# Attention and two feed-forward nets on one core: warm-up products on halves of TensorE's array

## The chip, the core and the metric

The kernel runs on one core of one Trainium2 chip. The metric is the device time of one execution in microseconds. Before the change it is 760.52 us, the median of three runs (759.41 to 760.74). Everything below is read from one further execution that was taken with the hardware profiler.

## What is computed

Three steps follow one another on 1152 tokens (2 x 576) of width 512. First, attention with 8 heads of 64 columns and a rotary embedding of q and k:

```python
def rotate(x):
    x1, x2 = (x[..., :half], x[..., half:])
    return np.concatenate([x1 * cos - x2 * sin, x1 * sin + x2 * cos], axis=-1)
q_rot, k_rot = (rotate(q), rotate(k))
scores = scale * np.matmul(q_rot, k_rot.transpose(0, 1, 3, 2))
...
attn = np.exp(scores)
attn = attn / (np.sum(attn, axis=-1, keepdims=True) + 1e-09)
return np.matmul(attn, v).astype(np.float32)
```

Then a mixture of 4 experts (512 to 1024, relu, back to 512), weighted by `domain_probs`, and last a net of 512 to 2048 to 512 with a leaky relu of slope 0.01.

## The kernel before

Attention goes over 8 pairs of heads. For each pair, the transposed q and k are loaded (L219), multiplied by the two tables `tab` (L229, two products), summed (L232), split into a rounded part (L268 on ACT, L270 on POOL) and a rest (L253, L255), and put together into `stk`. A score tile (L312) is a group of products into PSUM; DVE takes its negative maximum (L329), ACT the exponential (L339), TensorE turns it (L395, L401, L402), ACT and DVE split it (L420, L424), and it is multiplied with v (L472). Each multiplied operand is a sum of two float32r parts.

For the first pair the loads are cut in pieces so that work starts early: k in two halves of 288 columns, q in 192 and 384 columns. POOL and DVE share the rotary products and sums of these pieces.

Two small operands matter below. `VZ` holds, for two pairs in turn, the 64 left-over rows of v for both heads; it must be zero outside its blocks, so both are zeroed once (task `vz_zero`, L671, POOL), and the blocks are filled later (L284, L285). `stk` of the first pair needs zeros too (L316 on POOL, L317 on DVE). `ident` is the identity that turns tiles; POOL makes it first.

Nearly all instructions stand in tasks of a planner (`Plan`): each task names its engines, its cost and what it follows, and the planner writes down one order for each engine, which the engines then follow strictly. Waits between engines are put in from the tiles that instructions read and write: a write to a tile waits for all its earlier readers on other engines. What stands ahead of the planner in the code (`ident` and the warm-up products of TensorE, L629 to L631) stands ahead of its tasks in each engine's order too. The warm-up is `WARM` = 22 float32 products of `ident` with itself, into one PSUM tile that is not read:

```python
t = ps_a.tile([P, P], F32, tag="t", name="warm")
for _ in range(WARM):
    pe.matmul(t, lhsT=ident, rhs=ident, start=True, stop=True)
...
vz_zero = task("zero", 0, lambda e: [pool.memset(f32(z), 0.0) for z in VZ], [("POOL", 0.8)], ())
```

Of the kernel before, what the change touches and what calls it, by code (L numbers as in the profile page):

```python
# [11 lines left out]
F32 = mybir.dt.float32  # L12
# [8 lines left out]
P = 128  # L21
# [10 lines left out]
EARLY = 3  # L32
ON_DVE = (0, 1, 2, 3, 8, 9)
FH = FU // 2
WARM = 22


RANK = {"tab_q": [2043.63, 1989.1, 2043.63], "zero": [1293.68, 1391.39, 1354.79], "load_x1": [1391.71, 1675.91, 1893.96], "load_x0": [1434.91,
# [118 lines left out]
def f32(ap):  # L157
    return ap.bitcast(F32)
# [3 lines left out]
def attention_then_two_ffns(ctx, tc, xqk, vp, rope, dprob, w1, w2, w_in, w_out, out):  # L162
# [4 lines left out]
    pe, dve, act, pool, sp = nc.tensor, nc.vector, nc.scalar, nc.gpsimd, nc.sync  # L167
# [5 lines left out]
    ident = const.tile([P, P], F32, name="ident")  # L173
# [22 lines left out]
    def opened(name, bufs, **kw):  # L196
        return att.enter_context(tc.tile_pool(name=name, bufs=bufs, **kw))
# [5 lines left out]
    ps_s, ps_a, ps_b = (opened(n, 2, space=PSUM) for n in ("ps_s", "ps_a", "ps_b"))  # L203
# [5 lines left out]
    VZ = [tab_p.tile([P, 2, 2, D], F32R, name=f"vz{i}") for i in range(2)]  # L209
# [47 lines left out]
    def stack(p, w, h, part):  # L257

        stk, hl = stk_of(p), HL[p]
        src, dst = slice(64 * h, 64 * h + 64), slice(64 * part, 64 * part + 64)  # L260
        if w == 0:
            sp.dma_start(f32(stk[dst, h, 0]), f32(hl[src, part, 0]))
        else:
            sp.dma_start(f32(stk[dst, h, 1:3]), f32(hl[src, :, 1]))
# [30 lines left out]
    def chunk(i):  # L295
        return (0, i * P) if i < 2 else (0, 2 * P) if i == KT else (1, (i - 2) * P)
# [291 lines left out]
    def half_1(v, f, c):  # L588
        if (v, f) not in HP:
            HP[v, f] = ps_b.tile([P, 512], F32, tag="t", name=f"hp{v}_{f}")  # L590
        w, x = HW[v, 0], xT[0]
        for k, (l, r) in enumerate(((0, 1), (0, 0), (1, 0))):
            pe.matmul(HP[v, f], lhsT=w[:, c, l, f * P:(f + 1) * P], rhs=x[:, r, c], start=(c, k) == (0, 0), stop=(c, k) == (NC - 1, 2))  # L593
# [10 lines left out]
    def half_2(v, i):  # L604
        ps = HY[v, i] = ps_b.tile([P, DM], F32, tag="t", name=f"hy{v}_{i}")
        h, w, ts_ = HX[v], HW[v, 1], slice(i * P, (i + 1) * P)
        ops = []
        for f in range(FH // P):
            ops += [(h[:, 0, f, ts_], w[:, f, 1]), (h[:, 0, f, ts_], w[:, f, 0]), (h[:, 1, f, ts_], w[:, f, 0])]
        products(ps, ops)  # L610
# [15 lines left out]

    with tc.manual_schedule():

        t = ps_a.tile([P, P], F32, tag="t", name="warm")  # L629
        for _ in range(WARM):  # L630
            pe.matmul(t, lhsT=ident, rhs=ident, start=True, stop=True)  # L631
        plan = Plan()
        add = plan.add
        rings = {k: Ring(v) for k, v in {"x": 3, "hl": 1, "stk": 2, "v": 1, "vs": 2, "p": 2, "pl": 1, "s": 2, "ta": 2, "tb": 2, "pt0": 1, "pt1": 1,
# [17 lines left out]
        def task(kind, n, fn, choices, after):  # L652

            return add(fn, [(e, us, MORE[kind] if j else 0) for j, (e, us) in enumerate(choices)], after, rank_of(kind, n))
# [6 lines left out]
        def transfer(kind, n, fn, kb, after):  # L661
            return dma(fn, kb, after, rank_of(kind, n), 0.48 if "load" in kind else 0.65, MORE[kind] if kind in ("load_x0", "load_x1", "load_tab") and n < 1 else None)
# [20 lines left out]
        for p in range(NP_ALL):  # L683
# [4 lines left out]
            for w, nm in ((1, "xk"), (0, "xq")):  # L688
# [20 lines left out]
                for h in range(2 if p else 0):  # L709
                    for part in range(2):  # L710
                        t = transfer(f"stack{w}", n0 + .1 * h, lambda p=p, w=w, h=h, part=part: stack(p, w, h, part), 148 * (1 + w), lo_of[-1] + stk_w)
# [25 lines left out]
            for n in range(n0, n0 + PER):  # L737
                _, i, h = ORDER[n]
                big = i < KT
                c, _ = chunk(i)  # L740
# [75 lines left out]
        for v in range(2 * AHEAD):  # L816
# [13 lines left out]
            for f in range(FH // P):  # L830
                b_t, b_w = fresh("tb")
                t = None
                for c in range(NC):
                    need = [t] if c else parts[0][1] + x_done + b_w
                    t = task("half_1", 4 * v + f, lambda e, v=v, f=f, c=c: half_1(v, f, c), [("PE", 0.69)], need)
# [5 lines left out]
            for i in range(BLOCKS[0][1] // P):  # L841
                b_t, b_w = fresh("tb")
                t = task("half_2", 4 * v + 2, lambda e, v=v, i=i: half_2(v, i), [("PE", 1.37)], h_done + parts[1][1] + b_w)
# [311 lines left out]
        for c in (B11, T3, B21, B22):  # L1155
            d = plan.add(lambda e: None, [("X", 0.0 if c in (B11, T3) else 8.5, 0)], [], -99)
# [80 lines left out]
```

## Time and profile before

| | us |
|---|---|
| median of the runs | 760.52 |
| profiled execution | 759.67 |
| its span, first to last instruction | 757.7 |
| PE (TensorE products) busy | 728.2 (96%) |
| DVE busy | 527.0 (70%) |
| ACT busy | 422.0 (56%) |
| POOL busy | 385.9 (51%) |
| span granted at full TensorE clock, mean | 0.998 |

The busy shares are means over the whole span. Attention takes about its first 235 us, the two nets the rest. The engines' names: PE is TensorE, PEld its weight load, DVE VectorE, ACT ScalarE, POOL GpSimd, SP the engine that issues most transfers.

### The profile page before, as it was taken

The page shows a single profiled execution, that of the slowest core. Times are in us where ns is not written, and L with a number is a line of the kernel's source. Part 1 is how long each engine was busy: PE and PEld are TensorE (multiplying, and loading weights), DVE is VectorE, ACT ScalarE, POOL GpSimd, SP SyncE. Part 2 cuts the span into 40 slices and gives each one's busy share as a digit, 9 for nine tenths or more (in the row PEclk, how much of TensorE's full clock was granted, in tenths as well). Part 3 has the DMA queues.
Part 4 walks back from the last instruction along what each step waited for, and adds up shares of the span by engine and source line. Part 5 has one row for each costly group of instructions (what it writes and reads, how often), then busy time and mean ns, then how long its engine had stood idle before and what let it go on. Part 6 is the DMA issues. An engine that isn't in the chain of part 4 may idle for free.

```text
span 757.7 us, 12165 instructions
## 1 busy us (share of the span) xinstructions
PE 728.2 (96%) x4396; PEld 654.1 (86%) x4396; DVE 527.0 (70%) x927; ACT 422.0 (56%) x1017; POOL 385.9 (51%) x386
## 2 busy tenths in 40 slices
PE   6789899999999999999999999998999999999998
PEld 6678788888888988898998989888889899898997
DVE  7899988677776888986666666867769844243342
ACT  5688885666553464574472744735448447082540
POOL 7887876656267000246574763935004628475440
PEclk9999999999999999999999999999999999999999
DMA  8665646355042133454544533646101120000002
GB/s 261 166 189 168 158 106 173 114 140 122 29 167 93 47 112 97 138 172 138 158 144 146 190 128 91 202 153 220 58 1 57 33 80 29 28 29 1 1 29 97
DMA packets 40811, 84.55 MB, mean 112 GB/s; under 512 B 4656, under 2 KB 9520, under 8 KB 40752
## 3 DMA queue, kind: packets, MB, share of 16 engines
q1 hardware_dynamic: 39936, 83.00, 36.0%
q10 hardware_dynamic: 816, 0.79, 0.3%
q8 instruction: 34, 0.56, 0.3%
q14 instruction: 25, 0.20, 0.1%
HBM read 60.64 MB, written 10.75 MB: 94 GB/s over the span
## 4 chain that ended last, share of the span: by engine, by line
PE 85%; DVE 6%; POOL 3%; ACT 2%; DMA 2%; issue 1%; SPq 1%; ACTq 0%; POOLq 0%; DVEq 0%
PE start L472 35%; PE seeded L520 17%; PE start L520 12%; PE hp L593 4%; PE hy L472 4%; PE s L312 4%; PE o L472 3%; PE t L395 3%; PE seeded L527 1%; DVE pt L424 1%; DVE nm L329 1%; DMA x<-in_xqk_dram 1%; DMA tab<-in_rope_dram 1%; POOL x L232 1%; POOL hw L586 1%
## 5 line engine op out<-in xcount | busy, mean ns | idle before, releaser
L472 PE MATMUL start<-w,h 128*128 128x512 f32 (+1 forms) x1164 | 268.6, 388 | 0.0
L472 PEld LDWEIGHTS start<-w,h 128*128 128x128 f32 x1164 | 215.2, 188 | 42.9 <-DVE g L1024 0.2
L990 POOL TENSOR_TENSOR rest<-raw,rest 128x512 int32<-128x512 int32 x32 | 42.8, 1336 | 124.8 <-PE start L472 54.2
L914 POOL TENSOR_TENSOR h<-g,h 128x256 fp32r<-128x256 f32 (+1 forms) x64 | 53.9, 859 | 85.4 <-ACT h L1025 79.7
L268 ACT ACTIVATE w<-raw 128x512 fp32r<-128x512 f32 x81 | 50.3, 628 | 74.1 <-PE start L472 66.4
L914 POOL TENSOR_TENSOR w<-raw,w 128x512 fp32r<-128x512 f32 x46 | 64.0, 1401 | 41.0 <-ACT w L268 24.3
L520 PE MATMUL seeded<-xt,w 128*128 128x256 f32 (+1 forms) x480 | 74.3, 298 | 2.9 <-ACT seeded L1062 2.9
L520 PE MATMUL start<-xT,w 128*128 128x320 f32 (+1 forms) x480 | 74.7, 298 | 1.5 <-POOL w L914 0.9
L550 DVE SCALAR_TENSOR_TENSOR acc<-start,prob,acc 128x512 f32<-128x512 f32 x55 | 41.1, 749 | 48.0 <-PE start L472 47.9
L520 PEld LDWEIGHTS seeded<-xt,w 128*128 128x128 f32 x480 | 68.2, 189 | 4.4 <-ACT seeded L1062 3.7
L520 PE MATMUL seeded<-xT,w 128*128 128x320 f32 (+1 forms) x480 | 71.4, 298 | 0.5 <-ACT seeded L1062 0.5
L520 PEld LDWEIGHTS start<-xT,w 128*128 128x128 f32 x480 | 67.9, 190 | 2.6 <-POOL w L914 1.1
L520 PEld LDWEIGHTS seeded<-xT,w 128*128 128x128 f32 x480 | 67.2, 189 | 1.8 <-ACT seeded L1062 1.0
L420 ACT ACTIVATE pt<-t 128x384 fp32r<-128x384 f32 (+2 forms) x128 | 53.3, 440 | 25.6 <-PE t L395 22.4
L424 DVE TENSOR_TENSOR pt<-t,pt 128x384 fp32r<-128x384 f32 (+2 forms) x128 | 60.1, 492 | 8.7 <-ACT pt L420 7.2
L312 PE MATMUL s<-stk 128*128 128x288 f32 x288 | 53.3, 315 | 7.9 <-ACT p L339 5.4
L339 ACT ACTIVATE p<-s,nm 128x576 f32<-128x576 f32 x72 | 53.3, 740 | 13.0 <-DVE nm L329 12.4
L554 DVE TENSOR_TENSOR acc<-start,acc 128x512 f32<-128x512 f32 (+1 forms) x28 | 18.8, 673 | 54.5 <-PE start L472 54.5
L329 DVE TENSOR_REDUCE nm<-s 128x1 f32<-128x576 f32 x72 | 53.6, 749 | 4.0 <-PE s L312 3.3
L395 PE MATMUL t<-ident,p 128*128 128x128 f32 x288 | 45.4, 275 | 8.9 <-ACT p L339 3.4
L312 PEld LDWEIGHTS s<-stk 128*128 128x128 f32 x288 | 41.6, 192 | 12.1 <-ACT p L339 7.9
L1062 ACT ACTIVATE seeded<-seeded 128x320 f32<-128x320 f32 (+1 forms) x80 | 32.0, 400 | 33.0 <-PE seeded L520 32.1
(134 smaller groups left out, 1355.8 us busy)
## 6 DMA issues: line engine op xcount, KB each, us to landing
raw<-in_w_dram SPq DMA_DIRECT2D x32, 512.0 KB, 3.9
raw<-in_w_in_dram SPq DMA_DIRECT2D x16, 512.0 KB, 3.9
narrow<-rest SPq DMA_DIRECT2D x32, 256.0 KB, 3.0
raw<-in_w_out_dram SPq DMA_DIRECT2D x16, 512.0 KB, 3.7
raw<-narrow SPq DMA_DIRECT2D x16, 512.0 KB, 3.6
x<-in_xqk_dram SPq DMA_DIRECT2D x14, 576.0 KB, 6.4
stk<-hl SPq DMA_DIRECT2D x28, 288.0 KB, 5.4
hraw<-in_w_dram SPq DMA_DIRECT2D x12, 512.0 KB, 3.8
```

Of the source, the lines that this page charges most:

```text
L268: act.activation(out, x, AF.Copy, scale=by)
L312: pe.matmul(sc[:, c, :HS], lhsT=l, rhs=r[:, c * HS:(c + 1) * HS], start=(k == 0), stop=(k == len(ops) - 1))
L329: dve.tensor_reduce(out=NM[n], in_=SC[n][:, :, :HS], axis=AX.XY, op=ALU.max, negate=True)
L339: act.activation(PP[p, i][:, h].rearrange("p (c k) -> p c k", c=2), SC[n][:, :, :HS], AF.Exp, bias=NM[n], accum_out=SM[p][:, col:col + 1])
L395: pe.transpose(t[:, j], flat[:, b * P:(b + 1) * P], ident)
L420: act.activation(hi, src, AF.Copy)
L424: dve.tensor_tensor(out=lo, in0=src, in1=f32(hi), op=ALU.subtract)
L472: pe.matmul(ps, lhsT=l, rhs=r, start=(k == 0), stop=(k == len(ops) - 1))
L520: pe.matmul(out, lhsT=W1[a][:, l, c, fs], rhs=x_of(g, b, r, c), start=first and (c, k) == (0, 0), stop=(c, k) == (1, 2), skip_group_check= ...
L550: dve.scalar_tensor_tensor(out=acc, in0=ps, scalar=prob[:, t, e:e + 1], in1=acc, op0=ALU.mult, op1=ALU.add)
L914: return lambda e: eng[e].tensor_tensor(out=o, in0=a, in1=b, op=op)
L990: do(lambda e: pool.tensor_tensor(out=t, in0=low, in1=t, op=ALU.add), [("POOL", 1.35, 0, True)], due, [w, ("low", k)], [("rest", k)])
```

## The change

The 22 whole products of the warm-up become 4 whole ones, followed by pairs that each use half of the array: 3 pairs by rows (64 of the 128 contraction rows each, into two PSUM tiles), 3 pairs by output columns into one PSUM tile, 3 pairs by output columns into two PSUM tiles, all in float32 on `ident`; and 5 pairs by rows in float32r, with VZ[0] as both operands (128 columns of weights, 256 moving columns). For the latter VZ[0] is zeroed by a new memset ahead of them; the planner's task that zeroes both VZ stays.

```diff
-WARM = 22
+WARM = 4
...
-        t = ps_a.tile([P, P], F32, tag="t", name="warm")
+        warm = [ps_a.tile([P, 512], F32, tag="t", name=f"warm{i}") for i in range(2)]
+        pool.memset(f32(VZ[0]), 0.0)
+        one_r = VZ[0].rearrange("p h a d -> p (h a d)")
+        halves_ = [slice(0, 64), slice(64, P)]
+
+        def by_rows(w, x, times):
+            for _ in range(times):
+                for i, r in enumerate(halves_):
+                    pe.matmul(warm[i][:, :x.shape[1]], lhsT=w[r, :P], rhs=x[r], start=True, stop=True)
+
+        def by_columns(w, x, times, step):
+            for _ in range(times):
+                for i, r in enumerate(halves_):
+                    pe.matmul(warm[i * step][r, :x.shape[1]], lhsT=w[:, r], rhs=x, start=True, stop=True)
+
         for _ in range(WARM):
-            pe.matmul(t, lhsT=ident, rhs=ident, start=True, stop=True)
+            pe.matmul(warm[0][:, :P], lhsT=ident, rhs=ident, start=True, stop=True)
+        by_rows(ident, ident, 3)
+        by_columns(ident, ident, 3, 0)
+        by_columns(ident, ident, 3, 1)
+        by_rows(one_r, one_r, 5)
```

On POOL, the order from the making of `ident` to the first rotary work, before the change (`vz` is VZ, `x_1` and `x_0` are k and q of the first pair; in brackets what an instruction waits for):

```order
masks.py:197 MEMSET ident 128x128
L671 MEMSET vz_136 128x256
masks.py:199 ISA
masks.py:199 AFFINE_SELECT ident<-ident 128x128 [waits Pool_49]
L671 MEMSET vz_137 128x256
L316 MEMSET stk_179 64x1152 [waits Pool_49]
L229 TENSOR_TENSOR x_1_163<-x_1_163,tab 128x288 [waits DMAHW1_49,DMAHW0_49,Pool_49]
L229 TENSOR_TENSOR x_1_163<-x_1_163,tab 128x288 [waits DMAHW3_49,DMAHW2_49]
L229 TENSOR_TENSOR x_0_177<-x_0_177,tab 128x192 [waits DMAHW4_49]
L232 TENSOR_TENSOR x_0_177<-x_0_177 128x192 [waits DVE_49,Pool_49]
```

The zeroing of the first VZ stands between the two steps of `ident` here and waits for nobody. The same place on POOL in the changed kernel (L630 is the new memset, L689 the planner's task):

```order
masks.py:197 MEMSET ident 128x128
L630 MEMSET vz_136 128x256
masks.py:199 ISA
masks.py:199 AFFINE_SELECT ident<-ident 128x128 [waits Pool_49]
L689 MEMSET vz_136 128x256 [waits PE_49,Pool_49]
L689 MEMSET vz_137 128x256
L316 MEMSET stk_191 64x1152 [waits Pool_49]
L229 TENSOR_TENSOR x_1_175<-x_1_175,tab 128x288 [waits DMAHW1_49,DMAHW0_49,Pool_49]
L229 TENSOR_TENSOR x_1_175<-x_1_175,tab 128x288 [waits DMAHW3_49,DMAHW2_49]
L229 TENSOR_TENSOR x_0_189<-x_0_189,tab 128x192 [waits DMAHW4_49]
L232 TENSOR_TENSOR x_0_189<-x_0_189 128x192 [waits DVE_49,Pool_49]
```

The new memset has taken the old place of the first one, and the planner's first memset has moved behind `ident` and waits for PE. On TensorE, from the start to the first score tile (`s`), before the change:

```order
L631 MATMUL warm<-ident 128x128 [waits Pool_49]
L631 MATMUL warm<-ident 128x128 x21
L312 MATMUL s_218<-stk_179 128x288 [waits Activation_49,Pool_49]
L312 MATMUL s_218<-stk_179 128x288 [waits DVE_49]
L312 MATMUL s_218<-stk_179 128x288 x6
```

The warm-up waits for `ident` and the scores for three engines. The same place in the changed kernel, one pair of each kind shown (L637 by rows, L642 by columns):

```order
L645 MATMUL warm_140<-ident 128x128 [waits Pool_49]
L645 MATMUL warm_140<-ident 128x128 x3
L637 MATMUL warm_140<-ident 128x128
L637 MATMUL warm_141<-ident 128x128
L642 MATMUL warm_140<-ident 64x128 x7
L642 MATMUL warm_141<-ident 64x128
L637 MATMUL warm_140<-vz_136 128x256
L637 MATMUL warm_141<-vz_136 128x256
L312 MATMUL s_230<-stk_191 128x288 [waits Activation_49,Pool_49]
```

What follows on TensorE from the first score on has its old order; a float32 product stands as one row here and as two instructions in the trace.

## Rows read from the trace of the kernel before

**Rows 1.** The page's first line: the span and its instructions.

```profile
span 757.7 us, 12165 instructions
```

**Rows 2.** Chain that ended last, 0 to 45 us: start us, us, what.

```profile
1.48 5.94 DMA tab<-in_rope_dram
...
7.55 1.76 POOL x L229 x2
...
9.38 0.68 POOL x L232
...
26.11 1.82 POOL x L232
```

**Rows 3.** Timeline of PE to 20 us: start, us, instruction, [idle before, releaser].

```profile
1.57 7.79 PE L631 MATMUL warm<-ident 128*128 128x128 f32 x44 [1.57 <-POOL ident masks.py:199]
11.57 2.36 PE L312 MATMUL s<-stk 128*128 128x288 f32 x16 [2.22 <-POOL vz L285]
...
17.44 2.26 PE L312 MATMUL s<-stk 128*128 128x288 f32 x8 [0.26 <-DVE stk L321]
```

**Rows 4.** Timeline of POOL to 6 us.

```profile
1.46 0.31 POOL L671 MEMSET vz<- 128x256 f32 x1
1.83 1.05 POOL L316 MEMSET stk<- 64x1152 f32 x1
4.83 1.04 POOL L229 TENSOR_TENSOR x<-x,tab 128x288 f32<-128x288 f32 x1 [1.95 <-DMA tab<-in_rope_dram]
```

**Rows 5.** Timeline of DVE, 5 to 9 us.

```profile
5.91 0.46 DVE L232 TENSOR_TENSOR x<-x 128x288 f32<-128x288 f32 x1 [0.69 <-POOL x L229]
...
7.51 0.46 DVE L229 TENSOR_TENSOR x<-x,tab 128x288 f32<-128x288 f32 x1 [0.18 <-DMA tab<-in_rope_dram]
8.19 0.65 DVE L229 TENSOR_TENSOR x<-x,tab 128x192 f32<-128x192 f32 x1 [0.22 <-DMA x<-in_xqk_dram]
```

**Rows 6.** Timeline of ACT, 6 to 7 us.

```profile
6.40 0.44 ACT L268 ACTIVATE stk<-x 128x288 fp32r<-128x288 f32 x1 [1.38 <-DVE x L232]
```

**Rows 7.** Tile `warm`, 2.5 to 4 and 8 to 9.4 us: min/median/max ns, starts.

```profile
L631 PE MATMUL warm<-ident x9: 421/421/422, 2.2 to 3.9; 128*128 128x128 f32 x9
```

```profile
L631 PE MATMUL warm<-ident x13: 275/275/275, 7.7 to 9.1; 128*128 128x128 f32 x13
```

**Rows 8.** Timeline of PE: transposes that use 64 rows of the array.

```profile
23.00 0.51 PE L401 MATMUL t<-ident,p 64*128 64x64 f32 x7
...
23.41 0.22 PE L402 MATMUL t<-ident,p 64*64 64x64 f32 x1
...
48.47 0.46 PE L401 MATMUL t<-ident,p 64*128 64x64 f32 x4
```

**Rows 9.** Timeline of PE: float32r products of 256 columns.

```profile
46.32 0.63 PE L472 MATMUL o<-pt,vs 128*128 128x256 f32 x4
46.79 0.28 PE L472 MATMUL o<-pt,vz 128*128 128x256 f32 x1
```

**Rows 10.** Stretches: us, PE busy (instructions), granted clock, DMA share, GB/s.

```profile
16.00:18.00 2.00, 1.32 (x7) 0.82 0.36 39
18.00:20.00 2.00, 2.00 (x11) 0.50 0.92 266
```

**Rows 11.** Timeline of POOL, 14 to 46 us.

```profile
14.73 1.27 POOL L586 TENSOR_TENSOR hw<-hraw,hw 128x512 fp32r<-128x512 f32 x1
...
17.74 1.96 POOL L586 TENSOR_TENSOR hw<-hraw,hw 128x512 fp32r<-128x512 f32 x1
...
22.27 1.94 POOL L232 TENSOR_TENSOR x<-x 128x576 f32<-128x576 f32 x1
...
44.13 1.42 POOL L232 TENSOR_TENSOR x<-x 128x576 f32<-128x576 f32 x1
```

**Rows 12.** Timeline of DVE, 17 to 36 us: copies of L325.

```profile
17.68 0.21 DVE L325 CAST bd<-hl 64x128 fp32r<-64x128 f32 x1
...
32.99 2.17 DVE L325 CAST bd<-hl 64x128 fp32r<-64x128 f32 x2
```

## Prediction

> **What bounds the kernel now.** Three views were read: the page (the span), the chain of work that ended last, and the timelines of single engines over the first 30 us, since the change edits only what stands ahead of the plan. The profiled execution took 759.67 us around a span of 757.7 us [rows 1], 0.85 us under the median of the runs, 760.52. I work out a shift of the span and add it to the median.
>
> The reader should see in the chain [rows 2] that the start is not bound by TensorE. The chain begins with the load of `tab`, which lands at 7.4 us, and then stands on POOL without a gap of note until POOL's last rotary sum ends at 27.9 us; from there it goes to ACT and DVE. TensorE's warm-up runs from 1.57 to 9.36 us and the first real product, a score, starts at 11.57 [rows 3]: today the warm-up ends 2.2 us before anybody needs the engine. So its own length is free, but whatever touches POOL ahead of 7.55 us may not be.
>
> POOL has slack there: it zeroes VZ and the stack until 2.88, then waits 1.95 us for `tab`, multiplies once (4.83 to 5.87) and waits 1.68 us more [rows 4]. That is 3.6 us of cover.
>
> **The change part by part.** *The products.* 22 float32 products stay 22 (4 whole, 6 by rows, 12 by columns); ten float32r products of 256 columns are added. None of their results is read. Alone, all this would end before 11.57 us or little after it.
>
> *The wait.* The ten float32r products read VZ[0], zeroed ahead of them by one new memset on POOL (about 0.3 us, in the place in which VZ[0] was zeroed until now, so `ident` and the first warm-up product come when they did). But the plan still holds its own task that zeroes both VZ. Its first memset now overwrites what TensorE is still reading, and the order shows that it waits for TensorE. POOL works in order, so behind this wait stand the zeroing of VZ[1] and of the stack, the first rotary product, and all of POOL's chain. DVE's first sum waits for that rotary product, ACT for that sum, the scores for all three. SP's queue holds no new wait, but its later loads wait for these engines. The order is otherwise the same on all five engines (two waits of the first L527 products have changed places, since the PSUM banks rotate by one more; both producers are done long before).
>
> Call W the moment at which the last warm-up product is done. From it, step by step: wake-up 0.1 (my estimate, from hand-offs of 0.02 to 0.1 between neighbouring rows); VZ[0] again 0.37 (the step from one memset's start to the next [rows 4]); VZ[1] and the stack 1.42 (1.46 to 2.88 [rows 4]); the first rotary product 1.04 and a hand-off 0.05. That is W + 2.98. Then DVE adds 0.46 [rows 5], ACT rounds 0.44 [rows 6], DVE subtracts (0.46, as many columns as its sum), multiplies the second half 0.46 and the 192 columns of q about 0.45 (0.65 in the row, beside a busy POOL) [rows 5], with 0.12 for hand-offs: W + 5.37. POOL has done its own two rotary products by then (1.76 [rows 2], W + 4.75) and sums the 192 columns, 0.05 + 0.68 [rows 2]: W + 6.1. This sum ends at 10.06 today. From it on, everything in the chain follows in its old order and with its old durations, so the shift is **W - 4.0 us**. Until now DVE's work on the first half lay in POOL's second wait; that cover goes with the first one. I see nothing later that would swallow the shift: the loads on the chain are issued behind engines that are themselves shifted, and TensorE is full afterwards.
>
> *How long is W.* A whole float32 product is two instructions. They take 421 ns each early on and 275 ns later [rows 7]; their starts lie 0.213 us apart (8 steps from 2.2 to 3.9) and 0.117 us apart (12 steps from 7.7 to 9.1), so 0.43 us a product at the 1.2 GHz level and 0.23 us at 2.4 GHz. The change from the one to the other lies between these two stretches; instruction by instruction it is at 6.9 us. Does a pair on halves take the time of one product or of two? The trace has one place for rows: ten transposes that use 64 rows, five on each half, start between 23.00 and 23.41, 0.046 us apart, where four on one half alone, from 48.47, step by 0.08 us [rows 8]. So row pairs do overlap. No row has products on half the columns. Bounds: as one product per pair, or as two. I take one, since that is what the halves by rows show, the nearest row.
>
> The Trainium skill (TensorE: Matmul & The Clock Gate, Part 3: Packing small matmuls) says that row and column tiles both run concurrently and gives 2.38 times for three column tiles, which would make six column pairs cost hardly more than six products; the row half of it agrees with the transposes here, the column half no run here shows.
>
> With overlap: 4 + 3 + 6 = 13 products at 0.43 us, 5.6 us, from 1.57 with 0.15 for the first load: 7.3. A float32r product of 256 columns takes 0.117 us at the high clock (four steps from 46.32 to 46.79 [rows 9]), so five pairs take 0.6 us, or 1.2 at the low one; 0.2 for the last one's drain. W is 8.1 to 8.7; with a tenth for each change between whole, row and column products, **8.5**, and the shift **+4.5 us**. The floor, all of it at 2.4 GHz, is 1.57 + 0.15 + 13 x 0.23 + 0.6 + 0.2 = 5.5, a shift of +1.5.
>
> *The clock.* The clock was 0.82 on average in 16 to 18 us and 0.50 in 18 to 20 [rows 10]: after a stretch of a few transposes it fell to 1.2 GHz, and the third and fourth score tiles (from 17.44 and 19.50) ran slowly. In the changed kernel TensorE does nothing from about 8.5 to 16 us, so I expect the first two score tiles to run slowly instead, and those two at the high clock: an exchange, counted at nothing.
>
> **The rivals.** *The warm-up is longer.* If only row pairs overlap it is 4 + 3 + 12 = 19 products: slow until 6.9 (12 of them), 7 more at 0.23, W = 9.4; if no pair does, 22 products as today to 9.2, then ten at 0.117, W = 10.5. Shifts +5.4 and +6.5. If the clock also stays low throughout, these become 11.3 and 13.7, shifts +7.3 and +9.7. For it: no column row in the trace, and no row in which products on halves ran while the clock rose. Against: the row pairs.
>
> *The exchange of the clock fails*, and four score tiles run slowly. Sixteen scores took 2.36 us at the high clock and eight 2.26 at the low one [rows 3], 0.12 us more for each, 1.9 us for sixteen. Since the chain stands on POOL until 27.9 us, some of it may be hidden: 0.6 (a third) to 1.9 on top, 765.6 to 766.9. The Trainium skill (the same page, Why this matters for your kernels) warns of idle gaps between bursts of matmuls for just this loss; the fall at 17 us agrees.
>
> *Faster.* Operations on the chain are stretched where DVE and POOL work side by side: on POOL L586 took 1.96 us against 1.27 elsewhere, L232 1.94 [rows 11] and 1.82 [rows 2] against 1.42 [rows 11], on DVE two copies of L325 took 2.17 against 0.21 for one [rows 12]. That is 0.69 + 0.52 + 0.40 + 1.75 = 3.4 us. If the shift pulled the two engines' turns apart and all of this came back, it would outweigh the wait from W below 7.4; at the floor, W = 5.5, the result is 760.52 + 1.5 - 3.4 = 758.6. Against: it needs the high clock from the first product on, and DVE is held back by POOL itself, so their overlap moves along.
>
> *It does not wait as the order says*, or the shift is swallowed by slack that the chain hides: no change, 760.5.
>
> **How the numbers follow.** Forecast, pairs overlap, 50%: 760.52 + 4.5 = 765.0, its own range 763.7 to 766. Longer warm-up, 28%: 765.9 to 767.8, with a tail to 770.2. Slow scores on top, 13%: 765.6 to 766.9. No change 5%, faster 4%. Leaving out the tail, the last two cases and a little at the lower end, the range is 763.3 to 768.2. What a measurement of this kernel can tell from no change is about 0.2%, 1.5 us; all cases but the last two lie beyond it: slower 91%, same 5%, faster 4%.
>
> **What would show it.** POOL's memset at L689 should have some 6 to 7 us of idle time before it, ended by a warm-up product, and its first rotary product should start near W + 1.9 (10.4) rather than at 4.83; the 192-column sum near 14.6, the first score near 16 rather than 11.57. The starts within the warm-up tell which pairs overlap, and the granted clock under the first scores whether the exchange is one. It is wrong if POOL multiplies before the warm-up is over, or if the chain's later part begins less late than POOL does.

## The result and the profile after

The changed kernel takes 763.92 us, the median of four runs (763.47 to 765.18), beside 759.96 us for the kernel before in the same comparison (four runs): a ratio of 1.0056, with a 95% interval of 1.0037 to 1.0076. That is 4.0 us slower; 4.5 had been forecast, and the measured time lies in the forecast's own range, 763.7 to 766, too, near its lower end. Of the 1.1 us between 765.0 and 763.92, 0.56 is the kernel before, which took 759.96 in this comparison and not 760.52, and the rest is the shift. A second comparison on another occasion (e8 below) gives 764.39 against 760.62, 1.0048 [1.0030, 1.0065], 3.8 us.

The profiled execution took 763.47 us with a span of 761.4 us, 3.7 more than [rows 1]. POOL first, in its timeline (start, us, instruction, idle before it and what ended that):

```profile
0.87 0.32 POOL L630 MEMSET vz<- 128x256 f32 x1
...
8.37 0.56 POOL L689 MEMSET vz<- 128x256 f32 x2 [6.85 <-PE warm L637]
8.98 1.05 POOL L316 MEMSET stk<- 64x1152 f32 x1
10.12 2.30 POOL L229 TENSOR_TENSOR x<-x,tab 128x288 f32<-128x288 f32 x3
13.72 0.67 POOL L232 TENSOR_TENSOR x<-x 128x192 f32<-128x192 f32 x1 [1.30 <-DVE x L229]
```

The planner's zeroing of VZ, which stood at 0.87 and 1.46 us before, now waits 6.85 us for the last products of the warm-up (L637). The stack, zeroed at 1.83 in [rows 4], comes at 8.98, the first rotary product, there at 4.83, at 10.12, and the sum of the 192 columns of q at 13.72 instead of 9.38 [rows 2]: 4.34 us later. The work queued behind the one wait is what is late.

TensorE in the same stretch:

```profile
1.57 2.07 PE L645 MATMUL warm<-ident 128*128 128x128 f32 x8 [1.57 <-POOL ident masks.py:199]
3.57 1.65 PE L637 MATMUL warm<-ident 64*128 64x128 f32 x12
5.16 2.30 PE L642 MATMUL warm<-ident 128*64 128x128 f32 x24
7.38 0.85 PE L637 MATMUL warm<-vz 64*128 64x256 f32 x10
15.90 4.18 PE L312 MATMUL s<-stk 128*128 128x288 f32 x16 [7.67 <-POOL vz L285]
...
22.38 1.28 PE L312 MATMUL s<-stk 128*128 128x288 f32 x8
23.61 1.30 PE L312 MATMUL s<-stk,bd 128*128 128x288 f32 x8
...
30.74 2.29 PE L312 MATMUL s<-stk 128*128 128x288 f32 x8 [1.60 <-ACT p L339]
...
34.72 2.27 PE L312 MATMUL s<-stk 128*128 128x288 f32 x8
```

The warm-up has ended earlier, at 8.23 us instead of 9.36 [rows 3], although it holds ten products more, and yet the first score starts at 15.90 instead of 11.57. The sixteen products of the first two score tiles take 4.18 us (2.36 before), the sixteen of the third and fourth 1.28 and 1.30 (2.26 for the third alone before). The granted clock stands behind both. Stretches: us, their length, the busy time of PE, PEld, DVE, ACT and POOL, the granted clock (1.00 is 2.4 GHz, 0.50 is 1.2), the DMA share, GB/s:

```profile
10.00:12.00 2.00, 0.00 (x0) 0.00 (x0) 1.03 (x1) 0.00 (x0) 1.91 (x4) 0.54 1.06 407
...
16.00:18.00 2.00, 2.00 (x9) 2.00 (x10) 1.97 (x3) 1.44 (x3) 1.37 (x1) 0.50 0.54 150
18.00:20.00 2.00, 2.00 (x10) 1.86 (x10) 0.78 (x2) 1.00 (x3) 1.90 (x2) 0.50 0.85 265
22.00:24.00 2.00, 2.00 (x16) 1.84 (x16) 2.00 (x4) 1.84 (x4) 2.00 (x2) 1.00 0.73 205
30.00:35.00 5.00, 3.76 (x15) 3.34 (x16) 4.07 (x8) 3.01 (x8) 4.88 (x4) 0.57 0.50 104
```

While TensorE waits it falls to the 1.2 GHz level, it is there under the first scores and back at 2.4 GHz for the next ones, the exchange against [rows 10]. A second low stretch from 30 us on had not been forecast: two more score tiles, from 30.74 and 34.72, take 2.29 and 2.27 us, where the kernel before has 1.33 and 1.31 for its own from 26.40 and 29.93. So four score tiles run slowly, not two. Such a stretch is not the change's alone: the granted clock is also 0.50 from 28 to 32 us in two further executions of the kernel before (e7 and e9 below).

The shift can be followed with one instruction, DVE's last product of a pair of heads (L451), which stands 16 times in the attention stage. It is 4.55 us late at its first (42.51 against 37.96), 4.67 at the eighth, 3.43 at the ninth and 3.69 at the last; the span's 3.7 is the same number. So 4.3 us arise in the first 14 us, 0.3 are added by 111 us, and about 1 us comes back between 111 and 128 us. The place of that gain is a meeting of POOL and DVE. In the kernel before, POOL and DVE in turn:

```profile
121.10 1.42 POOL L229 TENSOR_TENSOR x<-x,tab_q 128x576 f32<-128x576 f32 x1
121.12 2.01 DVE L229 TENSOR_TENSOR x<-x,tab_q 128x576 f32<-128x576 f32 x1
```

and in the changed kernel:

```profile
125.69 1.95 POOL L229 TENSOR_TENSOR x<-x,tab_q 128x576 f32<-128x576 f32 x1
125.61 0.74 DVE L229 TENSOR_TENSOR x<-x,tab_q 128x576 f32<-128x576 f32 x1
```

Both multiply one half of a load by a table. Whichever starts first runs at its own pace and the other is held up: POOL ahead by 0.02 us makes DVE's product 2.01 us long, DVE ahead by 0.08 makes it 0.74 us, and DVE is what the chain needs there. The chain of the kernel before (start, us, what) stands on that product:

```profile
121.12 2.02 DVE x L229
```

In the changed kernel's first trace it is on TensorE's products at this place.

### The profile page after: what moved, and what is told of

It reads as the page before. It is cut to its first block, busy times and chain, and to the rows that moved or that the text cites. A ratio compares the mean times of both kernels' runs of the same rounds, so it can differ in the third digit from the quotient of the medians.

```text
span 761.4 us, 12187 instructions
## 1 busy us (share of the span) xinstructions
PE 729.8 (96%) x4406; PEld 655.5 (86%) x4406; DVE 525.5 (69%) x927; ACT 422.0 (55%) x1017; POOL 384.9 (51%) x387
## 4 chain that ended last, share of the span: by engine, by line
PE 86%; DVE 6%; POOL 3%; ACT 2%; issue 1%; DMA 1%; SPq 0%; POOLq 0%; ACTq 0%; DVEq 0%
PE start L472 34%; PE seeded L520 16%; PE start L520 12%; PE hp L593 4%; PE hy L472 4%; PE s L312 4%; PE o L472 4%; PE t L395 3%; PE seeded L527 1%; DVE nm L329 1%; DVE pt L424 1%; DMA x<-in_xqk_dram 1%; POOL x L232 1%; ACT p L339 1%; POOL hw L586 1%
## 5 line engine op out<-in xcount | busy, mean ns | idle before, releaser
L312 PE MATMUL s<-stk 128*128 128x288 f32 x288 | 56.1, 328 | 13.4 <-POOL vz L285 7.7
L312 PEld LDWEIGHTS s<-stk 128*128 128x128 f32 x288 | 44.2, 204 | 17.4 <-ACT p L339 8.2
```

Of the source, the lines that this page charges most:

```text
L312: pe.matmul(sc[:, c, :HS], lhsT=l, rhs=r[:, c * HS:(c + 1) * HS], start=(k == 0), stop=(k == len(ops) - 1))
```

## The experiments

Each edit is against the changed kernel, if nothing else is said. W is the end of the last warm-up product that reads VZ.

**Without the rewriting (e1).**

```diff
-        vz_zero = task("zero", 0, lambda e: [pool.memset(f32(z), 0.0) for z in VZ], [("POOL", 0.8)], ())
+        vz_zero = task("zero", 0, lambda e: [pool.memset(f32(z), 0.0) for z in VZ[1:]], [("POOL", 0.8)], ())
```

> The changed kernel, but the planner's task zeroes only the second VZ: the first is zeroed by the new memset already, and its blocks are first overwritten by L284, which starts at 10.0 us in the kernel before. Theory (the wait): the whole loss is POOL standing behind the warm-up, W - 4.0 us with W the end of the last product that reads VZ. No early wait is left, so the first rotary product of POOL starts at 4.8 us again, the first score near 11.5, and the time is that of the kernel before, 760.0 us within 0.2%. Rival (the products): the loss comes from the new products and the slow clock under the first scores; all of them are still there, so the time stays near 763.9 us.

Measured: 759.24 us against 759.66, ratio 0.9991 [0.9981, 1.0001]. All products of the change are there; only one memset of 0.3 us is gone, and with it its wait. POOL and TensorE:

```profile
4.84 1.04 POOL L229 TENSOR_TENSOR x<-x,tab 128x288 f32<-128x288 f32 x1 [1.97 <-DMA tab<-in_rope_dram]
```

```profile
7.70 0.85 PE L637 MATMUL warm<-vz 64*128 64x256 f32 x10
11.32 3.67 PE L312 MATMUL s<-stk 128*128 128x288 f32 x16 [2.77 <-POOL vz L285]
```

POOL multiplies at 4.84 again, long before the warm-up ends at 8.55. The whole loss is the wait; the products on halves cost nothing that can be measured, although the first scores still run slowly here, at 3.67 us.

**The pairs on VZ first (e3).**

```diff
+        by_rows(one_r, one_r, 5)
         for _ in range(WARM):
...
-        by_rows(one_r, one_r, 5)
```

> The changed kernel with the five float32r pairs on VZ at the head of the warm-up instead of at its end; the same products, the same rewriting of VZ. Theory (the wait): VZ is free at about 2.9 us (ten products at the low clock, half of them beside the other half), POOL has zeroed the stack by 4.6 us and multiplies at 4.8 as before; 760.0 us within 0.2%. Rival (the products): the work of TensorE is the same, so the time stays near 763.9 us.

Measured: 760.29 against 759.66, 1.0007 [0.9995, 1.0018]. The wait is still in the program, but it ends early:

```profile
2.81 0.56 POOL L689 MEMSET vz<- 128x256 f32 x2 [1.30 <-PE warm L637]
3.42 1.05 POOL L316 MEMSET stk<- 64x1152 f32 x1
4.80 1.05 POOL L229 TENSOR_TENSOR x<-x,tab 128x288 f32<-128x288 f32 x1 [0.33 <-DMA tab<-in_rope_dram]
```

Of POOL's 1.95 us of waiting for `tab` [rows 4], 0.33 are left, and the rotary product starts when it always did. The same wait costs nothing where POOL's own idle time covers it.

**Both members of a pair on one half (e4).**

```diff
-        halves_ = [slice(0, 64), slice(64, P)]
+        halves_ = [slice(0, 64), slice(0, 64)]
```

> The changed kernel, but both members of every pair lie on the same half of the array (rows 0 to 63, or columns 0 to 63), so nothing can run side by side; the same number of products of the same sizes. Theory: pairs on two halves overlap in the changed kernel; here they do not, the warm-up lasts until about 10.7 us instead of 8.2, POOL is released 2.5 us later, and the shift grows by the same 2.5 us up to 100 us of the run; at the end 765.5 to 767 us. Rival (no overlap, the pairs are as dear as single products): the warm-up ends at 8.2 us as before and the time stays at 763.9 us.

Measured: 768.9 against 759.66, 1.0116 [1.0101, 1.0131], 9.2 us: the direction is the theory's, the size more than it said. The products of the warm-up by tile (minimum, median, maximum in ns, first and last start), first the changed kernel:

```profile
L642 PE MATMUL warm<-ident x24: 272/418/473, 5.2 to 7.2; 128*64 128x128 f32 x24
...
L637 PE MATMUL warm<-ident x12: 417/418/579, 3.6 to 4.8; 64*128 64x128 f32 x12
...
L637 PE MATMUL warm<-vz x10: 275/276/381, 7.4 to 8.0; 64*128 64x256 f32 x10
```

then this one:

```profile
L642 PE MATMUL warm<-ident x24: 273/421/473, 6.4 to 10.8; 128*64 128x128 f32 x24
...
L637 PE MATMUL warm<-ident x12: 417/417/579, 3.6 to 6.1; 64*128 64x128 f32 x12
...
L637 PE MATMUL warm<-vz x10: 276/278/381, 11.0 to 12.2; 64*128 64x256 f32 x10
```

A single instruction takes as long in both, but on two halves the starts lie half as far apart: 0.11 against 0.23 us by rows, 0.09 against 0.19 by columns, 0.07 against 0.13 for float32r. Pairs overlap on all three kinds. That the column products of e4 write the same place of PSUM is not what holds them apart: those that write two tiles in turn step by 0.21 us at the low clock, like those that write one. Here the columns ran nearly all at the long durations of the low clock, so W is 12.4 instead of the 10.7 expected; POOL is released at 12.57, and L451 is late by 8.7 us at the first eight pairs and 7.6 at the end. The rule W - 4.0 gives 8.4 from the measured W; what I had wrong was when the clock would rise.

**22 whole products, then the pairs on VZ (e2).**

```diff
-WARM = 4
+WARM = 22
...
-        by_rows(ident, ident, 3)
-        by_columns(ident, ident, 3, 0)
-        by_columns(ident, ident, 3, 1)
```

> The warm-up of the kernel before (22 whole float32 products) and behind it only the five float32r pairs on VZ, with the rewriting of VZ. Theory (the wait): the float32 products end at 9.4 us, the pairs at about 10.1, the shift is 10.1 - 4.0 = 6.1 us up to 100 us of the run; 765 to 766.5 us at the end. Rival (the halves of the float32 products cost the time): they are gone, so the time falls below 763.9 us.

Measured: 765.7 against 759.66, 1.0071 [1.0055, 1.0087]. The clock rose early in the profiled execution (the products take about 275 ns from 5.1 us on, in the kernel before from 7.1), so W is 9.14, not 10.1; POOL is released at 9.28 and L451 is late by 5.2 at first and 4.4 at the end. Without one float32 product on a half of the array the loss is larger than with them, since the warm-up is longer.

**TensorE kept busy after POOL's release (e5).**

```diff
         by_rows(one_r, one_r, 5)
+        for _ in range(30):
+            pe.matmul(warm[0][:, :P], lhsT=ident, rhs=ident, start=True, stop=True)
```

> The changed kernel with 30 more whole float32 products on the identity behind the pairs on VZ, so that TensorE is busy from the release of POOL (8.2 us) to about 15.3 us, just ahead of the first score at 15.9. They read nothing that POOL writes. Theory (the start stands on POOL): the two score tiles now run at the high clock, 1.9 us sooner done, but POOL, released as before, sets the pace until 32 us; the time is that of the changed kernel within 0.5 us. Rival (the slow clock under the first scores is part of the loss): 1 to 2 us faster than the changed kernel.

Measured: 764.13 against 760.62, 1.0031 [1.0012, 1.0049], while the changed kernel itself gave 764.39 in the same comparison (e8).

```profile
8.69 6.96 PE L651 MATMUL warm<-ident 128*128 128x128 f32 x60
16.45 2.36 PE L312 MATMUL s<-stk 128*128 128x288 f32 x16 [0.79 <-POOL vz L285]
...
22.32 2.26 PE L312 MATMUL s<-stk 128*128 128x288 f32 x8
```

The first scores run at the high clock again, 2.36 us instead of 4.18, and start at 16.45, for POOL was released at 8.90 in this execution. Set beside e8, whose POOL was released at 8.90 too, the first L451 is late by 4.87 here and 5.03 there. The third score tile is the slow one again, as in the kernel before, and the second low stretch is gone too (1.00 from 30 to 36 us), so the difference is the price of all the slow scores that the change brought: 0.16 us at the first L451, 0.33 at the eighth, not 1 to 2. The two times alone, 0.3 us apart with intervals of more than a microsecond to each side, would not have settled this; the traces do.

**One warm-up product instead of 22 in the kernel before (e6).**

```diff
-WARM = 22
+WARM = 1
```

> The kernel before with one warm-up product instead of 22. Theory (the start stands on POOL): the first score tiles run at the low clock, which costs at most 1.9 us on TensorE and little on POOL's chain; 760 to 761 us. Rival (the warm-up carries the start): 762 us or more.

Measured: 760.58 against 760.62, 0.9998 [0.9976, 1.0020].

```profile
11.88 4.18 PE L312 MATMUL s<-stk 128*128 128x288 f32 x16 [9.52 <-POOL vz L285]
```

The scores are slow from the start, and the time is the same. What the change replaced was worth nothing that can be measured at this place, where POOL sets the pace.

**The same two kernels again (e7 to e12, none with an edit)**, to see whether the meeting near 121 us belongs to the change.

> The kernel before, unchanged, for a second trace. In the first trace POOL starts its L229 at 121.10 us, 0.02 ahead of DVE's at 121.12, and DVE's takes 2.01 us; in the changed kernel and in every variant so far DVE starts first by 0.02 to 0.08 and takes 0.74, and the shift is about 1 us smaller from there on. Theory (a coin of who starts first): the second trace may fall either way, and where DVE starts first, its later part comes about 1 us sooner than in the first trace. Rival (the warm-up decides it): POOL starts first here again.

> The changed kernel, unchanged, beside the others of this call: a second trace and more times. Expected near 763.9 us, POOL released near 8.3 us and shifted by 4.3 to 4.7 us up to 110 us of the run.

> The kernel before, unchanged, for a third trace of the meeting of POOL and DVE on L229 near 121 us. In two traces of it POOL started first by 0.02 us and DVE took 2.0 us. If the order of the two hangs on when their load lands (theory), POOL is first only where both are seen to start together, at the landing; if the kernel decides it (rival), POOL is first again in both further traces of before and DVE in both of the changed kernel.

> The changed kernel, unchanged, for a third trace of the same place. In two traces of it DVE started first and took 0.74 to 0.76 us, and the shift fell by about 1 us there. Theory and rival as for the kernel before.

> The kernel before, unchanged, for a fourth trace; theory and rival as for its third: by the theory POOL or DVE may be first, by the rival POOL is.

> The changed kernel, unchanged, for a fourth trace; theory and rival as for its third: by the theory POOL or DVE may be first, by the rival DVE is.

Measured times: e7 761.43 against 760.62, 1.0006 [0.9989, 1.0023]; e8 as above; single executions 760.83 (e9), 764.23 (e10), 758.88 (e11) and 763.78 (e12). In e8, POOL was released at 8.90 and the shift was 5.0, where 8.3 and 4.3 to 4.7 had been expected: the clock rose later. In the kernel before, POOL starts first in the first trace, e7 and e9 (and in e6), DVE in e11; in the changed kernel DVE in the first trace, e8 and e12, POOL in e10 (and in e5). POOL and DVE in e9, e11 and e10:

```profile
122.38 1.43 POOL L229 TENSOR_TENSOR x<-x,tab_q 128x576 f32<-128x576 f32 x1 [0.59 <-DMA x<-in_xqk_dram]
122.40 2.02 DVE L229 TENSOR_TENSOR x<-x,tab_q 128x576 f32<-128x576 f32 x1 [0.66 <-DMA x<-in_xqk_dram]
```

```profile
121.11 2.01 POOL L229 TENSOR_TENSOR x<-x,tab_q 128x576 f32<-128x576 f32 x1
121.07 0.76 DVE L229 TENSOR_TENSOR x<-x,tab_q 128x576 f32<-128x576 f32 x1
```

```profile
125.54 1.43 POOL L229 TENSOR_TENSOR x<-x,tab_q 128x576 f32<-128x576 f32 x1
125.56 2.02 DVE L229 TENSOR_TENSOR x<-x,tab_q 128x576 f32<-128x576 f32 x1
```

Both orders occur in both kernels, so the rival (the kernel decides) falls. Where the two are seen to wait for the load (e5, e7, e9), POOL is first by 0.02. From there on L451 gains 1.0 us on the first trace of before wherever DVE is first (e1, e2, e3, e4, e8, e11 and e12 besides the first trace of the changed kernel), and nothing where POOL is (e10: 4.43 and 4.45; e6 hardly; e5, e7 and e9 lose another 0.2 to 0.6, all three with a wait for the load).

What goes with the order is how long the load of `x` took that both multiply. From issue to landing, in us, first in the first trace of before, then in that of the changed kernel:

```profile
x<-in_xqk_dram SPq DMA_DIRECT2D x1, 576.0 KB, 7.4
```

```profile
x<-in_xqk_dram SPq DMA_DIRECT2D x1, 576.0 KB, 6.8
```

In all fourteen traces DVE is done with its instruction before (L447) 7.3 us after this load is issued. Where the load took 7.3 to 7.9 us (first trace of before, e5, e6, e7, e9, e10), POOL was first; where it took 5.0 to 7.2 (the other eight), DVE was. That is the theory of e9, put in numbers, though no run moved the load by itself. Whether the change makes the load shorter stays open: 7.2 to 7.9 us in the four traces of before and 6.5 to 7.3 in the four of the changed kernel overlap, and three of four against one of four is too few.

## Why the prediction was right, point by point

*What bounds the start.* Right. e1 and e3 give the time back by letting POOL go on early; e5 and e6 change the time of the first scores by 1.8 us each and move the whole by nothing that can be measured.

*The wait and what is queued behind it.* Right, and nearly step by step:

| step | forecast | trace of the changed kernel |
|---|---|---|
| W | 8.5 | 8.23 |
| POOL wakes | W + 0.1 | 8.37 = W + 0.14 |
| stack zeroed | W + 1.9 | 10.03 = W + 1.80 |
| DVE's first sum starts | W + 3.0 | 10.95 = W + 2.72 |
| q's 192 columns multiplied | W + 5.37 | 13.58 = W + 5.35 |
| their sum starts | W + 5.4 | 13.72 = W + 5.49 |
| shift | W - 4.0 | 4.34 = W - 3.9 |

Two terms were off and cancelled, as DVE and its neighbours show (DVE's timeline):

```profile
10.95 1.03 DVE L232 TENSOR_TENSOR x<-x 128x288 f32<-128x288 f32 x1 [5.67 <-POOL x L229]
12.48 0.46 DVE L253 TENSOR_TENSOR stk<-x,stk 128x288 fp32r<-128x288 f32 x1 [0.51 <-ACT stk L268]
12.86 0.72 DVE L229 TENSOR_TENSOR x<-x,tab 128x288 f32<-128x288 f32 x2
```

POOL's first product took 0.8 us instead of 1.04, with DVE idle; DVE's sum took 1.03 instead of 0.46, beside POOL's next product; and its two products took 0.72, not 0.91. Over the other executions, the first L451 is late by W - 3.7 to W - 3.9 (4.55 at 8.23, 5.03 at 8.77 in e8, 5.21 at 9.14 in e2, 8.71 at 12.44 in e4): the law holds over 4 us.

*How long W is.* Right, as one product per pair, for columns too, which no row of before had shown. The Trainium skill (TensorE: Matmul & The Clock Gate, Part 3: Packing small matmuls) says that column tiles run concurrently as row tiles do, and e4 agrees with 0.19 against 0.09 us a start. The tenths for changes between kinds are there: TensorE's weight loads idle 0.17 to 0.23 us at each. W itself was 8.23, 8.77, 8.21 and 8.77 in the four traces, as the products became short at about 6.6 us or at 7.9; that the forecast's 8.5 is their mean is in part luck.

*The clock.* Right in part. The first two score tiles changed places with the third and fourth as forecast, but two further ones ran slowly too, so it was no even exchange. Its price had been counted at nothing and is 0.16 to 0.33 us (e5). The low clock is dearer where TensorE is full: in e7 it was granted 0.50 from 95 to 98 us, with TensorE busy throughout, and the seventh L451 came 1.45 us later after the sixth than in the first trace of before.

*No later loss or gain.* This is the step that failed, by 1.0 us in the first trace: a place about 125 us after the start gave about a fifth of the shift back. One of the prediction's own signs of being wrong shows there, a later part (3.69 us) that is less late than POOL (4.34). The contention of POOL and DVE had been named, but as a rival that needed a short W; it is a meeting of two instructions that fell either way in either kernel, with the time of a load. Taken over four traces of each kernel, the changed one is late by 4.6 us at the first L451, 4.1 at the eighth and 3.4 at the last. Most of the first fall is the slow stretch of e7, in the kernel before; the second, 0.7 us, is the meeting. How much of that 0.7 is the change and how much the chance of four traces stays open. The difference between the forecast's 4.5 us and the measured 4.0 lies inside the interval of the measurement (2.8 to 5.8 us) and says nothing about it.

*The rivals.* A longer warm-up needs pairs that do not overlap; e4 is that case, at 768.9. Four slow score tiles did come, but they cost 0.16 to 0.33 us and not the 0.6 to 1.9 of the rival. No change and faster did not come.

## What to carry to other kernels

An operand borrowed for idle work is not free: whoever writes it next waits for the last reader, and everything queued behind that writer on its engine waits too. Read the price from the writer's queue, the end of the last read less the cover that the queue has, and not from the added work; one write less (e1) or an earlier read (e3) makes it nothing, and an operand of its own should do the same, which no run here shows. And before a warm-up is refined, look in the chain whether TensorE sets the pace at that place at all: here one product did as well as 22.

## What the runs showed of the hardware

Two halves of TensorE's array work side by side, by rows or by columns in float32 and by rows in float32r: the starts lie half as far apart as on one half (e4). Of two products on SBUF operands, one on POOL and one on DVE, the one that starts 0.02 to 0.09 us earlier takes its own time (1.42 or 1.43 us on POOL, 0.74 to 0.76 on DVE) and the other 1.95 to 2.02 us. The Trainium skill (SBUF — State Buffer, Who interferes with whom) says that issue order decides who blocks, and that a DVE instruction with two SBUF inputs contends with POOL's reads; these rows agree, and show that a few hundredths of a microsecond can move the end of a run by one.
